# Earlier transposes for the first four head pairs, and seven filler matmuls in the start-up of a fused attention and mixer kernel

## The chip, the cores and the metric

The kernel runs on one core of one Trainium2 chip. The metric is the device time of one execution in microseconds, as the median of several runs. The span of a profile, from the first to the last instruction of the core, is some 1.7 us shorter than the time of the same run.

## The reference

Four batches of eight heads with 768 rows of 64 go through block-sparse attention (a band, the outer blocks, and sampled blocks). The result is mixed over the tokens and then over the channels.

```python
scores = scale * np.matmul(q, k.transpose(0, 1, 3, 2))      # mask: blocks of 32
scores = np.where(mask, scores, -1000000000.0)
attn = softmax(scores)                                      # cut
x = (attn @ v) laid out as [B, S, H * D]                    # cut
u = x + (np.maximum(x^T @ w_tok1, 0) @ w_tok2)^T            # token mixing
out = u + np.maximum(u @ w_ch1, 0) @ w_ch2                  # channel mixing
```

## The kernel before

The program is written by a planner. Streams of matmuls and a list of operations for ScalarE and VectorE are placed in order of time by a cost model, and what comes out is one fixed order of instructions per engine. A stream with a lower number goes first. In the early part the planner adds a margin to some streams before it takes their inputs as ready:

```python
t = self.when(deps, tags)
...                                             # cut
if self.now < self.tight:                       # the first 40 us of the plan
    t += 300.0 if 1.5 < s[0] < 2.5 else 100.0 if s[0] == 1 else 0.0
```

The start-up is written by hand. Seven long matmuls on a constant keep TensorE busy while the first inputs arrive; then come the first transposes of pair 0, the mask rows (two matmuls of 24 x 24 x 384) and eight short fillers ahead of the first scores:

```python
for i in range(7):
    idle_mm()                                   # 512 columns each
...                                             # cut: masks, loads
first_lay(acopy, "q", 0)
qt0 = first_turn("q", 0)                        # three transposes
first_lay(acopy, "k", 0)
e2a, e2b = e2_mm(0, psM, "pm"), e2_mm(0, psO, "po")     # mask rows
kt0 = first_turn("k", 0)
for i in range(8):
    idle_mm(128)
```

Every later pair is loaded, laid out anew by VectorE (relayout), transposed by TensorE and copied out of PSUM. For pairs 1 to 3:

```python
lays = relayout(p)                              # klay, qlay, vaug: copies of priority 2 and 3
...                                             # cut: twelve transposes into PSUM
ev = P.op(("dve", "act"), {"dve": 550.0, "act": 740.0}, [last], evac, prio=2)
...
P.stream(0, qk_stream())                        # scores, then exp on ScalarE
P.stream(1, pv_stream())                        # PV: probabilities times values
P.stream(2, tr_stream())                        # transposes of all pairs
P.stream(1.7, first_tok_stream((0, 1, 2)))      # token mixing of batch 0
```

The softmax here doesn't subtract the row's maximum and nothing guards it: scores larger than these inputs give would overflow.

Of the kernel before, what the change touches and what calls it, by code (L numbers as in the profile page):

```python
# [25 lines left out]
def free(base_ap: bass.AP, extra_offset: int, dims) -> bass.AP:  # L26

    return bass.AP(
        tensor=base_ap.tensor,
        offset=base_ap.offset + extra_offset,  # L30
        ap=[list(base_ap.ap[0])] + [list(d) for d in dims],
    )
# [142 lines left out]
def kernel(  # L175
# [18 lines left out]
    NP = B * H // 2  # L194
# [6 lines left out]
    NT0 = 4  # L201
# [16 lines left out]
    P = Planner({"ps": 2, "po": 1, "pm": 3, "et": NET, "a_t": 2, "o": 3, "rc": 2,  # L218
                 "uT": 3})
# [3 lines left out]
    raws, arrive = {}, {}  # L223
# [92 lines left out]
    def idle_mm(n=512):  # L316
        nc.tensor.matmul(
            out=idle_ps[:, 0, 0:n], lhsT=free(one[:, 0:1], 0, [[0, 128]]),
            rhs=free(one[:, 0:1], 0, [[0, n]]), start=True, stop=True,
        )  # L320
# [68 lines left out]
    def first_lay(copy, nm, hf):  # L389
        copy(  # L390
            out=lay0[nm][:, 3 * hf : 3 * hf + 3, :, :],
            in_=f32[nm][:, :, 3 * hf : 3 * hf + 3, :].rearrange("p h c d -> p c h d"),
        )

    def first_turn(nm, hf):
        t = psM.tile([128, 3, 128], BF16, tag="pm", name=f"t{nm}first{hf}")
        for c in range(3):
            nc.tensor.matmul(
                out=t[:, c, :], lhsT=lay0[nm][:, 3 * hf + c, :, :].rearrange("p h d -> p (h d)"),
                rhs=ident[:, :], start=(c == 0), stop=(c == 2), is_transpose=True,  # L400
            )
        return t
# [8 lines left out]
    def e2_mm(hf, pool, tag):  # L411
        t = pool.tile([128, 512], FP32, tag=tag, name=f"pm_e2_{hf}")
        nc.tensor.matmul(  # L413
            out=t[R, 0:384], lhsT=t2add[R, :], rhs=indf[:, 384 * hf : 384 * hf + 384],
            start=True, stop=True,
        )
        return t
# [4 lines left out]
    vcopy, acopy = nc.vector.tensor_copy, nc.scalar.copy  # L422
    first_lay(acopy, "q", 0)
    qt0 = first_turn("q", 0)
    first_lay(acopy, "k", 0)
    e2a, e2b = e2_mm(0, psM, "pm"), e2_mm(0, psO, "po")
    kt0 = first_turn("k", 0)
    for i in range(8):
        idle_mm(128)
    first_evac(acopy, "q", 0, 0, qt0)  # L430
    first_evac(acopy, "q", 0, 1, qt0)
# [120 lines left out]
    kT_there, qT_there, va_there, qk_done, pv_done = {}, {}, {}, {}, {}  # L552
# [5 lines left out]
    def relayout(p):  # L558
        lays = {}
        for nm in ("k", "q", "v") if p else ("v",):  # L560
            raw = raws.pop((nm, p))
            arr = arrive.pop((nm, p))

            def emit(eng, nm=nm, raw=raw):
                if nm == "v":
                    nc.vector.tensor_copy(out=vaug[p % NV][:, :, :, 0:64], in_=raw)  # L566
                else:
                    lay = sbw.tile([128, NC, 2, D], BF16, tag=f"{nm}lay", bufs=2, name=f"{nm}lay{p}")
                    nc.vector.tensor_copy(
                        out=lay[:, :, :, :], in_=raw.rearrange("p h c d -> p c h d")  # L570
                    )
                    lays[nm] = lay

            deps = [arr]
            if nm == "v" and p >= NV:
                deps.append(pv_done[p - NV])
            if nm != "v" and p >= 3:
                deps.append(qT_there[p - 2, 1])
            if nm != "v" and p >= NPE:
                deps.append(quiet[sum(p > g for g in GATES)])  # L580
            if nm != "v" and p > NV + 4:
                deps.append(qk_done[p - NV + 1])
            lays[nm + "ev"] = P.op(("dve",), {"dve": 320.0}, deps, emit, prio=2 if nm != "v" else 3)
            copied[nm, p] = lays[nm + "ev"]
        va_there[p] = lays["vev"]
        return lays

    def crossbar(p):

        lays = relayout(p)  # L590
        for nm, bufs, there in (("k", ktb, kT_there), ("q", qtb, qT_there)):
            def emit(eng, nm=nm, bufs=bufs):
                nc.sync.dma_start_transpose(
                    out=bufs[p % NV][:, 0, :].rearrange("e (c s) -> e c s", c=NC),
                    in_=lays[nm][:, :, :, :].rearrange("p c h d -> p (c h d)"),
                )
            deps = [lays[nm + "ev"], mask_there, qk_done[p - NV]]
            ev = P.op(("sp",), {"sp": 1300.0}, deps, emit, prio=1, lat=4600.0)
            there[p, 0], there[p, 1] = ev, ev

    def transposes(p):
        yield lambda: ("v", p) in raws
        if p >= NPE:
            crossbar(p)
            return
        if p == 0:
            relayout(p)
            for nm in ("k", "q"):
                copied[nm, p] = Ev(START)
            for hd in range(2):  # L610
                kT_there[p, hd], qT_there[p, hd] = f_there["k", 1], f_there["q", 1]
            yield from first_rest()
            return
        for hd in range(2):
            kT_there[p, hd], qT_there[p, hd] = Ev(), Ev()
        lays = relayout(p)
        for nm, bufs, there in (("k", ktb, kT_there), ("q", qtb, qT_there)):
            box, last, rel = {}, Ev(), Ev()
            for c in range(NC):
                def emit(nm=nm, c=c, box=box, rel=rel):  # L620
                    if c == 0:
                        P.take("pm", rel)
                        box["t"] = psM.tile([128, NC, 128], BF16, tag="pm", name=f"t{nm}{p}")
                    nc.tensor.matmul(  # L624
                        out=box["t"][:, c, :],
                        lhsT=lays[nm][:, c, :, :].rearrange("p h d -> p (h d)"),
                        rhs=ident[:, :], start=(c == 0), stop=(c == NC - 1), is_transpose=True,
                    )
                deps = [lays[nm + "ev"]]
                if p >= NV:  # L630
                    deps.append(qk_done[p - NV])
                if p >= NT0:
                    deps.append(mask_there)
                yield 56.0, deps, [("pm", 1)] if c == 0 else [], emit, last if c == NC - 1 else None
            if p >= NT0:
                def evac(eng, buf=bufs[p % NV], box=box):
                    copy = nc.scalar.copy if eng == "act" else nc.vector.tensor_copy
                    copy(out=buf[:, 0, :], in_=box["t"][:, :, :].rearrange("p c s -> p (c s)"))

                ev = P.op(  # L640
                    ("dve", "act"), {"dve": 555.0, "act": 740.0}, [last, mask_there], evac, prio=2
                )
                for hd in range(2):
                    alias(there[p, hd], ev)
                alias(rel, ev)
                continue
            for hd in range(2):
                def evac(eng, hd=hd, buf=bufs[p % NV], box=box):
                    i = box["t"][64 * hd : 64 * hd + 64, :, :].rearrange("p c s -> p (c s)")
                    if eng == "act":  # L650
                        nc.scalar.copy(out=buf[0:64, hd, :], in_=i)
                    else:
                        nc.vector.tensor_copy(out=buf[0:64, hd, :], in_=i)

                ev = P.op(("dve", "act"), {"dve": 550.0, "act": 740.0}, [last], evac, prio=2)
                alias(there[p, hd], ev)
                if hd == 1:
                    alias(rel, ev)

    def alias(a, b):  # L660
        a.same_as = b
# [420 lines left out]
        for t in range(3):  # L1082
            x_there[p, t] = Ev()

    def tr_stream():
        for p in range(NP):
            yield from transposes(p)

    def tok_stream():
# [4 lines left out]
    def first_tok_stream(pairs):  # L1094
        for p in pairs:
            yield from tok_pair(p)
# [4 lines left out]

    P.stream(0, qk_stream())
    P.stream(1, pv_stream())
    P.stream(2, tr_stream())
    P.stream(1.7, first_tok_stream((0, 1, 2)))
    P.stream(0.5, first_tok_stream((3,)))
    P.stream(3, tok_stream())
# [100 lines left out]
```

## Time and profile before

| what | before |
|---|---|
| median of the first three runs | 258.02 us |
| the profiled run, its span | 255.23 us, 253.5 us |
| TensorE busy | 97% of the span |
| ScalarE, VectorE busy | 68%, 71% |

The views that carry the reading of the steady part are in the prediction. One more is needed here, TensorE's timeline of the start-up in the kernel before (start, length, engine, line, operation, operands, count, and the idle time before it with what ended it; PE is TensorE, ACT ScalarE, DVE VectorE):

```profile
3.96 0.53 PE L398 MATMUL tqfirst<-ident,qlay_first 128*128 128x128 bf16 x3
4.58 0.74 PE L413 MATMUL pm_e<-ktb,t2add 24*24 24x384 bf16 x2
5.25 0.34 PE L398 MATMUL tkfirst<-ident,klay_first 128*128 128x128 bf16 x3
5.43 0.63 PE L317 MATMUL ps_idle<-one 128*128 128x128 bf16 x8
6.35 0.89 PE L682 MATMUL ps<-qtb,ktb 88*128 88x256 bf16 x4 [0.29 <-DVE ktb L406]
```

The length of a group contains the latency of its last matmul (here a warm transpose alone takes 0.22 us, three take 0.34), so the pitch is read from lengths of like groups: three transposes take 0.53 us at 3.96 and 0.34 at 5.25. By the trace's single records their starts stand 0.107 us apart at 3.96 and 0.056 to 0.067 at 5.25; those of the 512-column fillers before them stand 0.427 apart from the second on. The clock of the array doubled between the two groups; the trace records the switch from half to full at 5.11. Between the first transposes and the mask rows at 4.58 there is a small hole: 0.09 us between the records, and some 0.3 us by the prediction's estimate that three transposes from 3.96 are through at 4.28.

### The profile page before, as it was taken

To read this page: it belongs to the slowest core of one execution; us is meant where nothing else is said; L and a number is where in the kernel's file an instruction comes from. 1 tells how busy PE (TensorE), PEld (TensorE's weight loads), DVE (VectorE), ACT (ScalarE), POOL (GpSimd) and SP (SyncE) were. 2 spreads that over 40 slices of the span, in tenths; PEclk is the share of its full clock that TensorE was granted. 3 is DMA by queue.
4 is the path that set the end of the run, shared out by engine and by line. 5 is a ranking of instruction groups with operands and counts; after the bars stand their busy time and mean duration, and the time that the engine had idled before them with its cause. 6 is when DMAs were issued, how large, how long until landed. Compare 5 with 4: busy or idle time off the path is not lost.

```text
span 253.5 us, 6661 instructions
## 1 busy us (share of the span) xinstructions
PE 244.9 (97%) x2777; PEld 159.2 (63%) x2796; DVE 179.8 (71%) x399; ACT 173.2 (68%) x214; POOL 51.4 (20%) x88
## 2 busy tenths in 40 slices
PE   7889999999999999999999999999999999999995
PEld 3579998566666556755676565557666744566444
DVE  6987666999898898998988989898998412200222
ACT  6799999968888577777896776676976310277100
POOL 8835985006740000082000000000000000000000
PEclk9999999999999999999999999999999999999999
DMA  6999999765995971279483313710400042300122
GB/s 153 183 215 202 212 203 206 129 79 86 161 201 90 172 161 67 52 120 187 72 127 65 63 45 79 131 73 12 100 9 1 3 103 83 124 3 0 41 111 99
DMA packets 44959, 26.77 MB, mean 106 GB/s; under 512 B 25408, under 2 KB 42064, under 8 KB 44928
## 3 DMA queue, kind: packets, MB, share of 16 engines
q0 software_dynamic: 15104, 12.98, 33.3%
q1 hardware_dynamic: 29552, 13.15, 23.0%
q8 instruction: 22, 0.36, 0.6%
q10 hardware_dynamic: 272, 0.20, 0.3%
q14 instruction: 9, 0.07, 0.1%
HBM read 26.74 MB, written 6.29 MB: 130 GB/s over the span
## 4 chain that ended last, share of the span: by engine, by line
PE 90%; DVE 3%; ACT 3%; issue 2%; ACTq 0%
PE pm_ch L1020 25%; PE pm_ch L1047 24%; PE ps L682 17%; PE po L776 14%; PE pm_tok L878 3%; ACT et L692 3%; PE pm_tok L853 3%; PE pm_tok_p L963 1%; PE pm_tok_p L940 1%; DVE qtb L420 1%; PE pm_e L413 0%; DVE vaug L566 0%; DVE dkf L357 0%; PE tk L624 0%; PE pm_ut L906 0%
## 5 line engine op out<-in xcount | busy, mean ns | idle before, releaser
L692 ACT ACTIVATE et<-ps 128x1024 bf16<-128x1024 f32 x144 | 138.9, 1023 | 32.4 <-PE ps L682 30.3
L1020 PE MATMUL pm_ch<-uT,w_ch 128*128 128x384 bf16 x384 | 74.1, 326 | 0.0
L700 DVE TENSOR_TENSOR et<-et,mask 128x1024 bf16<-128x1024 bf16 x108 | 70.2, 683 | 0.7 <-ACT et L692 0.6
L1047 PE MATMUL pm_ch<-w_ch,rc 128*128 128x512 bf16 (+2 forms) x293 | 66.1, 362 | 1.0 <-issue 0.5
L776 PEld LDWEIGHTS <-et 128*128 128x128 bf16 x1152 | 50.6, 97 | 17.3 <-issue 3.0
L776 PE MATMUL po<-vaug,et 128*128 128x65 bf16 x1152 | 57.0, 193 | 1.1 <-ACT et L692 0.4
L682 PE MATMUL ps<-qtb,ktb 64*128 64x256 bf16 (+1 forms) x576 | 55.5, 272 | 2.0 <-ACT et L692 1.1
L817 ACT ACTIVATE rc<-pm_ch 128x384 bf16<-128x384 f32 x58 | 28.5, 492 | 26.3 <-PE pm_ch L1020 26.0
L1020 PEld LDWEIGHTS <-w_ch 128*128 128x128 bf16 x384 | 33.7, 97 | 20.0 <-issue 3.4
L1047 PEld LDWEIGHTS <-rc 128*128 128x128 bf16 x312 | 27.4, 98 | 25.1 <-issue 1.7
L1059 DVE TENSOR_TENSOR o<-pm_ch,x 128x512 f32<-128x512 f32 x23 | 15.9, 690 | 38.5 <-PE pm_ch L1047 38.2
L682 PEld LDWEIGHTS <-ktb 64*128 64x128 bf16 (+1 forms) x576 | 28.8, 95 | 19.0 <-issue 13.3
L819 DVE TENSOR_SCALAR rc<-pm_ch 128x384 bf16<-128x384 f32 x38 | 21.1, 554 | 6.0 <-PE pm_ch L1020 5.5
L791 DVE TENSOR_TENSOR x<-po,recip 128x256 bf16<-128x256 f32 x48 | 20.4, 424 | 1.7
L790 DVE RECIPROCAL recip<-po 128x4 f32<-128x4 f32 x48 | 8.7, 180 | 13.8 <-PE po L776 13.5
L886 DVE TENSOR_TENSOR x<-pm_tok,x 128x512 bf16<-128x512 f32 x18 | 11.9, 683 | 1.2 <-PE pm_tok L878 1.1
L878 PE MATMUL pm_tok<-a_t,w_tok 128*128 128x256 bf16 x72 | 11.1, 277 | 0.2 <-DVE x L886 0.2
L1131 POOL COPY seen<-ktb 1x1 bf16<-1x1 bf16 x2 | 0.4, 180 | 50.7 <-DMA ktb<-klay 34.5
L853 PE MATMUL pm_tok<-x,w_tok 128*128 128x256 bf16 x72 | 9.8, 273 | 0.0
L878 PEld LDWEIGHTS <-w_tok 128*128 128x128 bf16 x72 | 7.5, 128 | 2.0 <-issue 1.4
L255 POOL DMA_DIRECT2D vraw<-in_v_dram x10 | 7.4, 742 | 3.2 <-DMA qraw<-in_q_dram 1.3
L535 POOL COPY mask<-maskb 128x240 bf16<-128x240 bf16 (+1 forms) x18 | 7.6, 495 | 0.0
(104 smaller groups left out, 138.6 us busy)
## 6 DMA issues: line engine op xcount, KB each, us to landing
out_dram<-o SPq DMA_DIRECT2D x17, 256.0 KB, 2.0
w_ch<-in_moe_w_ch_dram POOLq DMA_DIRECT2D x8, 384.0 KB, 9.8
vraw<-in_v_dram POOLq DMA_DIRECT2D x10, 192.0 KB, 6.9
kraw<-in_k_dram POOLq DMA_DIRECT2D x9, 192.0 KB, 6.9
qraw<-in_q_dram POOLq DMA_DIRECT2D x9, 192.0 KB, 6.8
out_dram<-o SPq DMA_DIRECT2D x13, 128.0 KB, 1.8
w_tok<-in_moe_w_tok_dram POOLq DMA_DIRECT2D x2, 384.0 KB, 10.6
ktb<-in_v_dram POOLq DMA_DIRECT2D x3, 192.0 KB, 8.5
```

Of the source, the lines that this page charges most:

```text
L682: nc.tensor.matmul(out=ps[:, hd, 256 * i : 256 * i + 256], lhsT=ktb[n][rows, h, 256 * jj + 128 * i : 256 * jj + 128 * i + 128], rhs=qtb[n] ...
L692: nc.scalar.activation(out=et[:, :, :], in_=ps[:, :, :], func=AF.Exp, scale=0.125)
L700: nc.vector.tensor_tensor(out=ets[s][:, :, :].rearrange("k h (i q) -> k h i q", i=2), in0=ets[s][:, :, :].rearrange("k h (i q) -> k h i q" ...
L776: nc.tensor.matmul(out=po[:, hd, c, :], lhsT=et[:, hd, 256 * i + 128 * c : 256 * i + 128 * c + 128], rhs=va[:, hd, 2 * jj + i, 0:65], star ...
L791: nc.vector.tensor_tensor(out=free(xs[b][:, pb // 2, 2 * t, 128 * (pb % 2) : 128 * (pb % 2) + 128], 0, [[64, 2], [256, 2], [1, 64]],), in0 ...
L817: nc.scalar.activation(out=o(), in_=i, func=AF.Relu)
L819: nc.vector.tensor_scalar(out=o(), in0=i, scalar1=0.0, scalar2=None, op0=ALU.max)
L853: nc.tensor.matmul(out=box["pm"][:, t, :], lhsT=w_tok1[:, sc, 128 * t : 128 * t + 128], rhs=xs[b][:, g, sc, :], start=(t == 0 and sc == 0) ...
L878: nc.tensor.matmul(out=ubox["pm"][:, i, :], lhsT=w_tok2[:, t, :, 2 * s2 + i], rhs=a_t[:, t, :], start=(i == 0 and t == 0), stop=(i == 1 an ...
L1020: nc.tensor.matmul(out=pbox["pm"][:, 0:384], lhsT=w_ch1[:, dmc, 128 * cc : 128 * cc + 128], rhs=st[b]["uT"][:, dmc // 2, 3 * sh : 3 * sh + ...
L1047: nc.tensor.matmul(out=pbox["pm"][:, 0:n], lhsT=box["rc"][:, cc, 128 * sc : 128 * sc + 128], rhs=w_ch2[:, cc, lo : lo + n], start=(cc == 0 ...
L1059: nc.vector.tensor_tensor(out=o[:, :].rearrange("p (g e) -> p g e", g=2), in0=pbox["pm"][:, :].rearrange("p (g e) -> p g e", g=2), in1=st[ ...
```

## The change

The intent is to have the transposed pairs ready earlier, by moving transposes ahead of PV and their copies ahead of relayouts, and to close two small holes of the start-up with fillers. The condition on pair p-2 only keeps the two transpose streams in order.

```diff
     qt0 = first_turn("q", 0)
+    for i in range(3):
+        idle_mm(128)
     first_lay(acopy, "k", 0)
 ...
-    for i in range(8):
+    for i in range(12):
         idle_mm(128)
 ...
-        yield lambda: ("v", p) in raws
+        yield lambda: ("v", p) in raws and (p < 2 or (p - 2, 1) in qT_there)
 ...
-                ev = P.op(("dve", "act"), {"dve": 550.0, "act": 740.0}, [last], evac, prio=2)
+                ev = P.op(("dve", "act"), {"dve": 550.0, "act": 740.0}, [last], evac, prio=1.5)
 ...
-    P.stream(2, tr_stream())
+    P.stream(0.7, tr_stream(range(NT0)))
+    P.stream(2, tr_stream(range(NT0, NP)))
```

(NT0 is 4. The stream function takes the pairs as its argument; that hunk is cut.)

More of the change, by code (lines that the diff above doesn't have):

```diff
@@ L653, in evac @@
                         nc.vector.tensor_copy(out=buf[0:64, hd, :], in_=i)
-                ev = P.op(("dve", "act"), {"dve": 550.0, "act": 740.0}, [last], evac, prio=2)
+                ev = P.op(
+                    ("dve", "act"), {"dve": 550.0, "act": 740.0}, [last], evac, prio=1.5
+                )
                 alias(there[p, hd], ev)
@@ L1083, with tr_stream @@
             x_there[p, t] = Ev()
-    def tr_stream():
-        for p in range(NP):
+    def tr_stream(pairs):
+        for p in pairs:
             yield from transposes(p)
```

## The prediction

> **What bounds the kernel now.** I read three views in this order: the chain of work that ended last (which engine sets the end), the busy time by stretch (where that engine is not full), and the timelines of ScalarE, TensorE and VectorE around the emptiest stretch (what it waits for there).
>
> The chain, by engine, and then the stretches; the columns are the stretch in us, its length, and the busy us of each engine with its number of instructions:
>
> ```profile
> PE 90%; DVE 3%; ACT 3%; issue 2%; ACTq 0%
> ```
>
> ```profile
> 7.28:12.00 4.72, 3.75 (x47) 2.46 (x44) 4.42 (x10) 4.07 (x5) 4.00 (x6) 1.00 1.20 179
> 12.00:18.00 6.00, 5.58 (x100) 5.09 (x97) 5.21 (x14) 5.62 (x7) 2.89 (x4) 1.00 1.17 214
> 18.00:24.00 6.00, 5.57 (x92) 4.99 (x91) 4.52 (x13) 5.91 (x7) 3.08 (x5) 1.00 1.30 200
> 24.00:30.00 6.00, 6.00 (x106) 5.68 (x104) 3.20 (x10) 6.00 (x7) 5.14 (x12) 1.00 1.21 209
> ...
> 48.00:54.00 6.00, 5.66 (x67) 3.38 (x66) 5.72 (x16) 5.19 (x7) 0.00 (x0) 1.00 0.27 49
> 54.00:100.00 46.00, 45.59 (x567) 28.82 (x570) 41.01 (x88) 35.83 (x44) 11.63 (x17) 1.00 0.85 133
> 100.00:200.00 100.00, 99.01 (x1205) 63.68 (x1213) 86.38 (x179) 75.11 (x90) 7.29 (x11) 1.00 0.39 73
> ```
>
> TensorE is the bound: 90% of the chain is its matmuls, and from 54 to 200 us it is busy 99%. Its work is a fixed sum, so a change of order can only win what TensorE idles. Between 7.28 and 54 us that is 2.2 us (46.72 us less the 44.51 us busy in the stretches between these marks), nearly all of it before 24 us and in 48 to 54 us. The whole prize of reordering the first four pairs is therefore about 2 us, 0.8% of 258.
>
> The first four pairs run one exponential (exp) after another on ScalarE, with the matmuls fitted between. ScalarE's timeline (start, length, engine, line, operation) shows one hole:
>
> ```profile
> 11.91 4.94 ACT L692 ACTIVATE et<-ps 128x1024 bf16<-128x1024 f32 x5 [0.18 <-PE ps L682]
> 16.74 0.79 ACT L651 COPY ktb<-tk 64x768 bf16<-64x768 bf16 x1
> 17.86 4.71 ACT L692 ACTIVATE et<-ps 128x1024 bf16<-128x1024 f32 x5 [0.34 <-PE ps L682]
> ```
>
> The ninth exp, the last of pair 0, ends at 16.85; the tenth, the first of pair 1, starts at 17.86. That is 1.01 us without an exp. A transpose copy (0.79 us) lies in it, but does not make it: ScalarE then still waits 0.34 us for scores. TensorE and VectorE say why the scores are late:
>
> ```profile
> 15.85 0.65 PE L776 MATMUL po<-vaug,et 128*128 128x65 bf16 x16
> 16.91 0.42 PE L776 MATMUL po<-vaug,et 128*128 128x65 bf16 x8 [0.41 <-ACT et L692]
> 17.16 1.04 PE L682 MATMUL ps<-qtb,ktb 88*128 88x256 bf16 x8
> ```
>
> ```profile
> 10.16 0.58 DVE L566 COPY vaug<-vraw 128x768 bf16<-128x768 bf16 x1
> 10.78 0.55 DVE L488 COPY qtb<-qtb 24x1536 bf16<-24x1536 bf16 x1
> 11.36 0.59 DVE L569 COPY klay<-kraw 128x768 bf16<-128x768 bf16 x1
> ...
> 12.71 0.43 DVE L569 COPY qlay<-qraw 128x768 bf16<-128x768 bf16 x1
> 13.07 0.29 DVE L521 TENSOR_SCALAR maskb<-pm_mask 128x144 bf16<-128x144 f32 x1
> 13.32 1.12 DVE L653 COPY ktb<-tk 64x768 bf16<-64x768 bf16 x2
> ...
> 15.67 1.13 DVE L653 COPY qtb<-tq 64x768 bf16<-64x768 bf16 x2
> ```
>
> Pair 1's last transposed q is in place only at 16.80. Expecting that, the planner put the last eight PV matmuls of pair 0 ahead of pair 1's first scores; those eight wait for the ninth exp, so nothing of pair 1 can be scored before 17.16.
>
> [...]the scores at 17.16 stand behind a PV group that began to wait 0.41 us earlier. [...]the seven 512-column fillers from 1.00 take 3.17 us (about 0.43 each with the last one's tail), and later transposes stand 0.056 us apart. The new fillers are to be judged by that. [...]
>
> **The change, part by part**, with the order of instructions of both programs laid side by side.
>
> 1. Fillers: three more 128-column matmuls after the first q transposes, four more before the first scores. Before, TensorE is idle 0.1 us before the first mask-row matmul (4.58) and 0.29 us before the first scores (6.35). Three cold fillers are 3 x 0.107 = 0.32 us from about 4.29 (three transposes from 3.96 at 0.107), so until 4.61: the mask rows may go 0.03 us later. Four warm ones, 4 x 0.056 = 0.22, fit the 0.29. Cost 0 to 0.05 us. If they brought the warm clock forward, the two mask-row matmuls would gain at most 0.3 us (384 columns, 3 x 0.107 = 0.32 each, halved); I give that little weight, since TensorE was all but full there already.
>
> 2. Pair 1 earlier. VectorE's new order is row copy, vaug, maskb, klay, qlay, two ktb copies, reciprocal and normalisation, two qtb copies. With the start-to-start times of before: the row copy at 10.16 (+0.58), vaug 10.74 (+0.62), maskb 11.36 (+0.25), klay 11.61 (+0.59), qlay 12.20 (to 12.63). The k transposes are split around a score group on TensorE and end near 13.2; ktb copies 13.3 (+1.04), reciprocal and product (+0.56) to 14.9, qtb copies (1.13) to 16.0. So pair 1 stands at about **16.0 instead of 16.8**, and its first scores now follow a PV group whose exp is long done. They issue at about 16.1, and the tenth exp starts as the ninth ends, at about 16.85: **1.0 us earlier**. The hole of 0.18 at 11.9 may close too, since the fifth score group of pair 0 now goes ahead of sixteen PV matmuls that it stood behind; but one k transpose waits for klay (12.2) ahead of the next score group, which may open 0.15 again. I count these as nil.
>
> 3. Copies ahead of relayouts: ScalarE no longer does the 0.79 us copy; VectorE does it (0.55). That is no further gain, the copy lay in the hole already counted. In exchange four eviction ReLUs go from ScalarE to VectorE (58 and 38 become 54 and 42).
>
> 4. What reaches the end. The channel mixing can start once pair 3 is token-mixed, in the trace at 50.23; from there TensorE is full. In the new order it starts after the 45th score group, not the 44th. One group more costs about 0.96 us of exp rhythm (17 in 16.30 us), so the start is near 50.23 - 1.0 + 0.9 = about 50.1. But the extra score group (0.33 us of TensorE by start-to-start) and eight to sixteen more PV matmuls (0.25 to 0.5) are then done. Sum: 0.1 + 0.33 + 0.4 = 0.8, to which the 0.26 us wait at 49.3, perhaps filled by the extra work, could add. I take **0.9 us**: 258.02 - 0.9 = 257.1.
>
> **Rivals.** *The hole moves instead of closing*: transposes now stand in TensorE's queue ahead of PV and without the planner's margin of 0.3 us, so a late relayout blocks scores as well. For it: klay and qlay stand behind vaug and maskb, and VectorE is 5.21 of 6 us busy there. Against: half a microsecond of slack by step 2. It would leave 257.5 to 258.2. *Transfers set the pace*: the input queues move some 200 GB/s until 48 us, and VectorE waited 1.3 us for pair 3's k at 21.39. Against: pair 3 is scored only at 34, so the exps have slack; 0.2 us lost at most. *VectorE becomes the bound later*: it is 86% busy from 100 to 200 us and gets some 2.8 us more (four ReLUs at 0.55 and a copy). Against: TensorE idles only 1 us in those 100 us. *The plan shifts everywhere*: every later step is placed anew, with other transfers in between; TensorE idles some 1.4 us in 54 to 200 now, and a redraw can add or save as much. This is the largest term of the range, and the likeliest way to see no gain. *Everything idle goes*: 2.2 us, 255.8, is the floor.
>
> **Range and chances.** Centre 257.1; downward to the floor, 255.8; upward, the gain lost and 0.5 us of new stalls on top, 258.5. Faster by 2% would need 5.2 us, over twice the idle time there is; slower by 2% needs as much in new stalls, which only a badly wrong plan gives. Hence 0.02, 0.96, 0.02.
>
> **What would show it.** Right: in ScalarE's timeline the tenth exp starts at 16.7 to 17.1 with no copy in the exp phase; pair 1's qtb copies end near 16.0; TensorE's idle time from 12 to 24 us falls from 0.85 to under 0.4; 54 to 200 us stays as full as before. Wrong: a wait of a score group for a relayout or a transposed copy near 12 to 16 us, an exp hole elsewhere before 50 us, a start of channel mixing after 50.3, or more than 2 us of TensorE idle in 54 to 200. A gain over 2 us would mean that busy TensorE time hid more slack than its records show.

## The result, and the profile after

The changed kernel took 254.41 us (median of four runs, 254.26 to 255.08); before, beside it, took 258.03 (257.66 to 259.83). The ratio is 0.9851 with a 95% interval of 0.9802 to 0.9900. A ratio is always the mean time of one kernel's fast runs over that of the other's in the same rounds, so it is not quite the ratio of the medians. That is 3.6 us, four times the predicted 0.9 and below the predicted range. Chance made it larger: none of these four runs of before was a quick one, where 16 of all 46 are (table below). The mean of all 46 is 257.44, against 254.94 for all ten runs of the changed kernel, 2.5 us apart.

The two profiles tell another tale: the spans are 253.5 and 252.6 us, 0.9 apart. First the busy time by stretch of the changed kernel, in the columns of the prediction's table:

```profile
12.00:18.00 6.00, 5.68 (x103) 5.21 (x100) 5.03 (x14) 5.92 (x8) 2.86 (x4) 1.00 1.18 215
18.00:24.00 6.00, 6.00 (x106) 5.52 (x103) 5.04 (x14) 6.00 (x7) 3.24 (x5) 1.00 1.30 201
...
48.00:54.00 6.00, 6.00 (x58) 3.43 (x57) 5.71 (x15) 5.42 (x9) 0.00 (x0) 1.00 0.40 44
54.00:100.00 46.00, 45.73 (x559) 27.84 (x562) 41.27 (x88) 32.99 (x39) 11.13 (x17) 1.00 0.80 136
100.00:200.00 100.00, 99.52 (x1212) 63.25 (x1217) 87.19 (x182) 75.45 (x90) 6.81 (x11) 1.00 0.38 72
```

TensorE idles 0.32 us from 12 to 24 us, where it idled 0.85, and 0.75 us from 54 to 200, where it idled 1.40. ScalarE's timeline of the changed kernel has no hole and no copy from the second exp on:

```profile
7.51 1.02 ACT L696 ACTIVATE et<-ps 128x1024 bf16<-128x1024 f32 x1 [0.99 <-PE ps L686]
9.11 41.87 ACT L696 ACTIVATE et<-ps 128x1024 bf16<-128x1024 f32 x44 [0.57 <-PE ps L686]
```

VectorE's last copies for pair 1, in the changed kernel, end at 16.09 instead of 16.80:

```profile
14.96 1.13 DVE L655 COPY qtb<-tq 64x768 bf16<-64x768 bf16 x2
```

And TensorE's start-up in the changed kernel, with the new fillers:

```profile
4.29 0.53 PE L317 MATMUL ps_idle<-one 128*128 128x128 bf16 x3
4.74 0.81 PE L413 MATMUL pm_e<-ktb,t2add 24*24 24x384 bf16 x2
5.49 0.50 PE L398 MATMUL tkfirst<-ident,klay_first 128*128 128x128 bf16 x3
5.78 0.95 PE L317 MATMUL ps_idle<-one 128*128 128x128 bf16 x12
6.59 0.89 PE L686 MATMUL ps<-qtb,ktb 88*128 88x256 bf16 x4
```

Here the array is still at half clock at 5.49 (three transposes in 0.50 us; the trace records the switch at 5.94), so in this run the first scores are even 0.24 us later than in the profiled run of before. So the profiles show the reordering at work, and a gain of 0.9. The other 2.7 us lie between the profiled run of before (255.23) and its usual runs (258). Something differs from run to run of one and the same program.

### The profile page after: what moved, and what is told of

Its sections match the earlier page's. It is cut to its first block, busy times and chain, and to the rows that moved or that the text cites.

```text
span 252.6 us, 6684 instructions
## 1 busy us (share of the span) xinstructions
PE 246.2 (97%) x2786; PEld 158.6 (63%) x2803; DVE 182.5 (72%) x404; ACT 169.8 (67%) x209; POOL 50.1 (20%) x88
## 4 chain that ended last, share of the span: by engine, by line
PE 95%; DVE 2%; ACT 2%; issue 1%
PE pm_ch L1024 25%; PE pm_ch L1051 24%; PE ps L686 17%; PE po L780 15%; PE pm_tok L882 4%; PE pm_tok L857 3%; ACT et L696 2%; PE ps_idle L317 1%; PE pm_tok_p L967 1%; PE pm_tok_p L944 1%; PE pm_ut_p L990 1%; DVE qtb L420 1%; PE tq L626 1%; DVE ktb L406 1%; PE tk L626 1%
## 5 line engine op out<-in xcount | busy, mean ns | idle before, releaser
L1024 PE MATMUL pm_ch<-uT,w_ch 128*128 128x384 bf16 x384 | 73.0, 326 | 0.1
L780 PEld LDWEIGHTS <-et 128*128 128x128 bf16 x1152 | 48.1, 97 | 14.3 <-issue 3.8
L780 PE MATMUL po<-vaug,et 128*128 128x65 bf16 x1152 | 55.2, 193 | 0.2
L821 ACT ACTIVATE rc<-pm_ch 128x384 bf16<-128x384 f32 x54 | 26.6, 492 | 25.7 <-PE pm_ch L1024 25.6
L1051 PEld LDWEIGHTS <-rc 128*128 128x128 bf16 x312 | 28.0, 98 | 24.6 <-issue 0.2
L823 DVE TENSOR_SCALAR rc<-pm_ch 128x384 bf16<-128x384 f32 x42 | 23.3, 554 | 5.9 <-PE pm_ch L1024 5.2
```

Of the source, the lines that this page charges most:

```text
L780: nc.tensor.matmul(out=po[:, hd, c, :], lhsT=et[:, hd, 256 * i + 128 * c : 256 * i + 128 * c + 128], rhs=va[:, hd, 2 * jj + i, 0:65], star ...
L821: nc.scalar.activation(out=o(), in_=i, func=AF.Relu)
L823: nc.vector.tensor_scalar(out=o(), in0=i, scalar1=0.0, scalar2=None, op0=ALU.max)
L1024: nc.tensor.matmul(out=pbox["pm"][:, 0:384], lhsT=w_ch1[:, dmc, 128 * cc : 128 * cc + 128], rhs=st[b]["uT"][:, dmc // 2, 3 * sh : 3 * sh + ...
L1051: nc.tensor.matmul(out=pbox["pm"][:, 0:n], lhsT=box["rc"][:, cc, 128 * sc : 128 * sc + 128], rhs=w_ch2[:, cc, lo : lo + n], start=(cc == 0 ...
```

## The experiments

All kernels below gave correct results. Each list of runs is in the order of time. All are labelled fast but for some at 259.2 us or more, which are called slow only because they lie over 1.5% above the fastest run of the same kernel; on one core there is no second die to compare with. A call that held quick runs of before thus loses its slowest from the ratio, so I compare levels of single runs and not the ratios.

The theories: **A**, the reordering saves, and the fillers only pad; **B**, the fillers decide when TensorE gets its full clock, which usual runs of before get late. The later texts call B the clock theory.

### Fillers alone, and the reordering alone (first call)

Before plus both groups of fillers:

```diff
+    for i in range(3):
+        idle_mm(128)
-    for i in range(8):
+    for i in range(12):
```

> The kernel before with both groups of fillers (3 and 4 more) and nothing else. Theory A, the reordering is what saves: no change, 257.5 to 258.5 us. Theory B, the fillers bring TensorE to its full clock reliably, and a usual run of before (258.0, against 255.2 in its one profiled run) misses it: 254.8 to 255.6 us, the time of that profiled run.

Measured: 255.40, 255.31, 255.27, 256.69. Before in the same rounds: 259.66, 254.83, 259.85, 254.91, 258.24, 258.13, 255.14. Theory A's 258 is out. The fillers take away the upper levels without any reordering.

The changed kernel minus the same seven fillers (the diff above, reversed):

> The changed kernel without its seven new fillers: the reordering alone. Theory A: 254.2 to 254.8 us, as the whole change. Theory B: 256.5 to 257.5 us, 1 us under before, since the profiles differ by 0.9 us in span.

Measured: 255.17, 255.07, 257.14, 256.69; neither theory's numbers fit all four. The profiled run (255.17) shows why. Its stretches between 12 and 16 us have the granted clock in the third column from the end:

```profile
12.00:14.00 2.00, 2.00 (x21) 1.75 (x19) 0.16 (x2) 1.18 (x2) 1.42 (x3) 0.50 1.29 199
14.00:16.00 2.00, 1.68 (x23) 1.36 (x21) 1.77 (x5) 1.54 (x3) 1.05 (x2) 0.93 1.10 244
```

TensorE had its full clock from 4.06 us (the transposes there take 0.36 us instead of 0.53) and fell back to half from 10.88 to 14.30, for 3.4 us (score groups take 1.06 us at 12.24 and 0.60 at 14.97). So there are two ways to lose: a late warm-up, and a relapse. The mean clock of a run gives the relapses away: 0.993 is 0.007 x 253 us at half lost, so 1.8 us lost or 3.5 us at half clock. (A mean of 0.998 need not be a relapse: in the result's profile it is the fall at 251.70, just before the end.)

The kept traces hold the times of the clock's switches, which the views do not print. In fifteen of the 17 the first switch lies between 3.64 and 6.97 us; in the two late ones it lies at 16.56 and 20.40. It differs from run to run of one program: the two profiles of before itself have it at 5.11 (the first one) and at 3.64 (the one of the third call). What sets it was not shown.

Before plus the three fillers in the first hole only:

```diff
     qt0 = first_turn("q", 0)
+    for i in range(3):
+        idle_mm(128)
```

> The kernel before with the three fillers between the first transposes and the mask rows alone. Theory A: 257.5 to 258.5 us. Theory B with the gap of 0.1 us before the mask rows as the culprit: near 255.3 us; with the gap before the first scores as the culprit: still 258.

Measured: 254.75, 255.49, 254.77, 254.90.

Before plus the four fillers ahead of the first scores only:

```diff
-    for i in range(8):
+    for i in range(12):
```

> The kernel before with the four fillers before the first scores alone (12 in place of 8). Theory A: 257.5 to 258.5 us. Theory B: near 255.3 us if the gap before the first scores (0.29 us) is the culprit, 258 if it is the one before the mask rows.

Measured: 258.25, 255.56, 260.09, 254.98. The three fillers after the first transposes are the ones that matter; the other four leave the levels as they were. The profiled run of this kernel fell on a late one (258.25), and TensorE's timeline shows it at work:

```profile
5.61 1.49 PE L317 MATMUL ps_idle<-one 128*128 128x128 bf16 x12
...
14.49 1.03 PE L682 MATMUL ps<-qtb,ktb 88*128 88x256 bf16 x4
15.32 0.85 PE L624 MATMUL tk<-ident,klay 128*128 128x128 bf16 x6
...
17.33 0.60 PE L682 MATMUL ps<-qtb,ktb 88*128 88x256 bf16 x4
```

A score group takes 1.03 us at 14.49 and 0.60 at 17.33; between them, by the trace at 16.56, the clock came. Before it the score groups of four take 1.01 to 1.06 us and six transposes 0.85 (at 15.32; 0.50 at 18.63), and between the exps from 7.99 to 17.12 ScalarE waits 0.18 to 1.00 us for scores. The clock column says 1.00 for the stretches from 0 to 18 us all the same, so this late warm-up must be read from the lengths.

### Which part does what (second call)

The changed kernel with 8 in place of 12 fillers before the first scores:

```diff
-    for i in range(12):
+    for i in range(8):
```

> The changed kernel with the three gap fillers but 8 instead of 12 fillers before the first scores. The gap fillers alone on before measured 254.8, both groups 255.3, so if the four tail fillers cost 0.5 us by delaying the first scores: 253.8 us, all runs within 1.3 us. If the tail fillers help to keep the clock: 254.4 with some runs over 256.

Measured: 254.22, 257.01, 254.43, 255.41, with clocks of 0.999, 0.987, 1.000 and 0.993. A miss: the best run is not better than with 12, and there were two relapses, of some 6.6 us at half clock (257.01) and 3.5 (255.41) by these means. With four runs it can't be told whether the four fillers made the difference.

The changed kernel with 6 in place of 7 long warm-ups, so that the hole moves ahead of the first transposes:

```diff
-    for i in range(7):
+    for i in range(6):
         idle_mm()
```

> The changed kernel with 6 in place of 7 long warm-up fillers, which leaves TensorE idle for some 0.4 us before the first transposes. Theory clock [...]: the slow runs return, several of four at 256.5 us or more, with matmuls at the doubled pitch beyond 6 us. Rival, the fillers only pad and the spread is chance: 254.2 to 254.6 in all runs, as nothing waits for the seventh filler.

Measured: 255.25, 257.96, 257.77, 255.09. All other fillers and the reordering are in place, and nothing waits for the seventh warm-up; still half the runs are back at 258. This is what theory B said of the times. The doubled pitch beyond 6 us was not seen, as the profiled run (255.25) was a quick one: a hole of 0.16 us before the first transposes, full clock from 4.10, and a relapse from 10.93 (mean clock 0.993, so some 3.5 us at half; a score group takes 1.06 us at 12.21 and 0.60 at 14.97).

The changed kernel with only the transposes moved, copies at their old priority:

```diff
-                    ("dve", "act"), {"dve": 550.0, "act": 740.0}, [last], evac, prio=1.5
+                    ("dve", "act"), {"dve": 550.0, "act": 740.0}, [last], evac, prio=2
```

> The changed kernel with the transposes ahead of PV, but their copies at the old priority. The order up to pair 1's copies is that of the whole change, so the hole before the tenth exp closes: 254.2 to 254.6 us if this half of the reordering saves the 1.0 us; 255.3 if the copies' priority does.

Measured: 255.28, 255.99, 255.27, 255.84. The hole before the tenth exp is closed, and yet nothing is won. ScalarE's timeline of this kernel:

```profile
9.11 21.08 ACT L696 ACTIVATE et<-ps 128x1024 bf16<-128x1024 f32 x22 [0.56 <-PE ps L686]
30.50 1.94 ACT L696 ACTIVATE et<-ps 128x1024 bf16<-128x1024 f32 x2 [0.31 <-PE ps L686]
32.60 10.64 ACT L696 ACTIVATE et<-ps 128x1024 bf16<-128x1024 f32 x11 [0.16 <-PE ps L686]
43.76 8.36 ACT L696 ACTIVATE et<-ps 128x1024 bf16<-128x1024 f32 x9 [0.52 <-PE ps L686]
```

Three holes of together 0.99 us open later in the same exp phase. Channel mixing starts at 50.66, against 49.80 in the changed kernel. The gain was given back before it reached the end.

The changed kernel with only the copies moved, transposes at the old priority:

```diff
-    P.stream(0.7, tr_stream(range(NT0)))
+    P.stream(2, tr_stream(range(NT0)))
```

> The changed kernel with the copies ahead of relayouts, but the transposes at the old priority behind PV. The order up to pair 1's copies is that of before, so the hole of 1 us stays: 255.3 us, as with the fillers alone; 254.4 if the copies' priority is what saves.

Measured: 256.56, 255.96, 256.03, 255.55, all with clock 1.00. The old hole is there, and channel mixing starts only at 51.50. In the profiles of this call and of the changed kernel, only both halves together keep the exps without a hole. Why these four runs differ by 1 us at a full clock I did not find out.

### The relapses, and the levels themselves (third call)

The changed kernel with eight more fillers where TensorE waits 0.67 us for an exp, ahead of the fourth score group. To be tested is whether the relapses come from this wait. The wait in TensorE's timeline of the changed kernel:

```profile
10.19 0.90 PE L686 MATMUL ps<-qtb,ktb 88*128 88x256 bf16 x4 [0.67 <-ACT et L696]
```

The edit:

```diff
         p, t, jj = s
+        if s == (0, 1, 0):
+            hole = psO.tile([128, 512], FP32, tag="po", name="po_hole")
+            for i in range(8):
+                nc.tensor.matmul(out=hole[:, 0:128], lhsT=<ones>, rhs=<ones>, start=True, stop=True)
         P.take("ps", rel)
```

> The changed kernel with eight more fillers in the hole of 0.67 us before the fourth score group of pair 0, where TensorE waits for an exp. Theory clock: the relapses to half clock after the warm-up (runs at 255.1 us with a mean clock of 0.993, 257.0 with 0.987) [...]; with it filled all runs are at 254.2 to 254.7 with clocks of 0.998 or more. Rival, relapses have another cause: one to three of six runs at 255 to 257 us, as before.

Measured: 254.83, 254.69, 254.94, 254.60, 255.12, 255.06; all clocks 0.999 or 1.000. TensorE's timeline of this kernel, where the wait for the exp has shrunk to 0.21:

```profile
9.35 0.63 PE L682 MATMUL po_hole<-one 128*128 128x128 bf16 x8
10.19 0.90 PE L693 MATMUL ps<-qtb,ktb 88*128 88x256 bf16 x4 [0.21 <-ACT et L703]
```

The changed kernel itself in the same rounds:

> The changed kernel itself, for the share of its levels: most runs at 254.2 to 254.6 us, a few at 255 to 257 with a clock of 0.985 to 0.994 [...], none with a late warm-up.

Measured: 254.53, 255.55, 254.87, 255.42, 255.51, 255.34, with clocks of 0.999, 0.993, 1.000, 0.992, 0.992, 0.993. Four of six runs relapsed, by their clocks for some 3.5 to 4 us at half, and took 255.3 to 255.6, where the two without took 254.5 and 254.9. I had expected a few. With the hole filled none of six did. No late warm-up in either, as expected.

Before without its seven warm-ups:

```diff
-    for i in range(7):
+    for i in range(0):
         idle_mm()
```

> The kernel before without its seven long warm-up fillers, so that TensorE starts cold and with holes. Theory clock: every run has a late full clock and lands with the slow runs of before or worse, 257.5 to 261 us, with matmuls at the doubled pitch to 10 us or beyond. Rival, the two levels of before (255 and 258 to 260) have nothing to do with the warm-up: still two levels, some runs at 255.

Measured: 259.99, 259.66, 259.24, 259.72. The two levels are gone, and what is left is the upper one, with transposes still at the long pitch at 19 us (three in 0.51 us; the first switch is at 20.40). The upper level of before, 259.3 to 259.9, lies where a start without any warm-up lies.

Before itself:

> The kernel before itself, for the share of its levels: half the runs at 254.6 to 255.3 us, the others at 257.7 to 258.3 or 259.5 to 259.9. If the profiled run is one of the slow ones, its trace shows matmuls at the doubled pitch until beyond 12 us and the same order of waits after that.

Measured: 257.68, 257.96, 259.37, 258.73, 258.08, 259.25; no quick run among six, against half expected. The profiled run (257.68, clock 0.987) was not the late warm-up that I expected but one that relapsed for 6.8 us:

```profile
10.00:12.00 2.00, 2.00 (x25) 1.63 (x25) 1.40 (x3) 1.40 (x2) 1.43 (x2) 0.62 1.31 199
12.00:14.00 2.00, 2.00 (x23) 1.61 (x22) 1.09 (x4) 1.18 (x2) 1.43 (x2) 0.50 1.28 191
14.00:16.00 2.00, 2.00 (x26) 1.75 (x24) 1.50 (x4) 1.09 (x2) 0.73 (x2) 0.50 1.15 254
16.00:18.00 2.00, 2.00 (x26) 1.71 (x24) 0.44 (x3) 1.34 (x2) 0.70 (x1) 0.68 1.11 200
```

Half clock from 10.47 to 17.29, and ScalarE (fourth engine) busy 1.1 to 1.4 of every 2 us: its exps waited for scores. A busy TensorE here is a slow one, not a productive one: score groups take 1.04 us at 14.70 and 0.60 at 17.63. So no late warm-up of before itself was profiled: for its other slow runs it is read from their mean clocks, which show no relapse, and from the profile of the kernel with the late fillers.

### The reordering at a settled clock (fourth call)

What was left open is the reordering's own worth, as all comparisons so far mix clock phases. With all three holes filled in both, before and the changed kernel:

```diff
 (the kernel before)
+    for i in range(3):                     # after the first q transposes
+        idle_mm(128)
-    for i in range(8):
+    for i in range(12):                    # before the first scores
+        if s == (0, 1, 0):                 # and the eight into po_hole, as above
```

> The kernel before with all fillers of the change and the eight more in the hole before the fourth score group: the old order at a settled clock. If the reordering is worth 0.9 us on its own: 255.7 us, 0.9 above the next run. If it is worth 0.4 or less: 254.9 to 255.3. No run over 256.5 either way, as the clock theory has no late warm-up and no relapse here.

Measured: 254.66, 255.26, 255.37, 255.36, 254.76, 254.74 (mean 255.03).

The changed kernel with the same holes filled, the file of the third call again:

```diff
 (the changed kernel)
+        if s == (0, 1, 0):                 # the eight into po_hole, as above
```

> The changed kernel with the same eight fillers (e9 again, for the same rounds): 254.6 to 255.1 us in all runs.

Measured: 254.74, 255.12, 254.97, 254.52, 255.00, 254.59 (mean 254.82). No run of either relapsed or warmed up late. The reordering is worth **0.2 us** here, the difference of two means whose runs spread by 0.6 to 0.7; it is not clear of zero. In the profiled runs both spans are 253.0. The changed order (the last run named) shows a hole which its first profile did not have, in ScalarE's, TensorE's and VectorE's timelines:

```profile
31.56 19.83 ACT L703 ACTIVATE et<-ps 128x1024 bf16<-128x1024 f32 x21 [0.56 <-PE ps L693]
```

```profile
30.61 0.42 PE L787 MATMUL po<-vaug,et 128*128 128x65 bf16 x8 [0.40 <-DVE x L802]
```

```profile
26.35 0.70 DVE L571 COPY klay<-kraw 128x768 bf16<-128x768 bf16 x1
...
28.46 1.54 DVE L568 COPY vaug<-vraw 128x768 bf16<-128x768 bf16 x2
```

The relayouts, which now come after the copies, fall between 26 and 30 us. There they take twice as long as elsewhere or longer: klay 0.70 us instead of 0.35, and the two vaug copies 1.54 instead of 0.62 at 20.01. The normalisation after them comes late, PV waits 0.40 us for it, and the scores behind PV wait too. In the first profile of the changed kernel the same copies were a little shorter (0.55, and 1.44 for the two) and the hole did not open; GpSimd spreads the masks there from 25.80 to 28.48 and issues loads from 28.43 to 30.59. Whether the copies are long because of GpSimd's work was not tested.

This hole sets a limit to the 0.2. It stands near 31 us in all three profiles of the changed order with the eight fillers (0.56, 0.56 and 0.61 us; spans 253.1, 253.0 and 253.0) and in none of the three at full clock without them (spans 252.6, 252.8 and 252.5). The old order's shortest spans are 253.1 with the gap fillers and 253.0 with all. So 0.2 is the worth of the reordering beside the eight fillers; by the profiles without the hole it is some 0.2 to 0.6. Whether the eight fillers open the hole was not tested.

The last run also drops the four fillers ahead of the first scores:

```diff
-    for i in range(12):
+    for i in range(8):
```

> The same with 8 in place of 12 fillers before the first scores. If the four tail fillers delay the first scores where the full clock comes late (first scores at 7.02 instead of 6.59 us in two profiles): 0.1 to 0.4 us under the run before. If they are needed for the clock: some runs at 255.4 or more with a clock under 0.995.

Measured: 254.73, 253.65, 254.53, 255.03, 254.57, 254.26 (mean 254.46), no clock under 0.998. It is 0.36 us below the run before, as expected, though the runs of this one spread by 1.4, so this is not clear of the noise. By its mean it is quicker than before (254.46 against 256.67 for the eleven runs of before in these rounds) and than the changed kernel (254.94 over its ten runs, of two other calls): the version to keep, if one had to choose.

### All runs together

| kernels | runs | 253.6 to 257.2 us | 257.6 us and more |
|---|---|---|---|
| before | 46 | 16 | 30 |
| no warm-ups at all | 4 | 0 | 4 |
| before with the four late fillers only | 4 | 2 | 2 |
| six warm-ups | 4 | 2 | 2 |
| the reordering without fillers | 4 | 4 | 0 |
| seven warm-ups and the three gap fillers, in either order | 54 | 54 | 0 |

The four runs of the reordering without fillers leave a rival, that the reordering alone takes the upper level away. Its two runs at 256.69 and 257.14, with clocks of 0.999, may be late warm-ups that cost less in this order, and neither was profiled. That the reordering does not keep the upper level away is shown by the kernel with six warm-ups, which contains it and has two of four runs there.

## Why the prediction was right or wrong, point by point

**The starting point** was the first mistake. The text subtracted 0.9 us from 258.02, the median of the timed runs, after reading all of its idle times from a run of 255.23. The two numbers stood side by side. A profiled run that is 2.8 us quicker than the others is a run in which something that costs 2.8 us is missing; the bound on the prize ("about 2 us, 0.8% of 258") was read from a trace that did not contain the loss.

**The fillers** are the step that failed, in its own words: "If they brought the warm clock forward, the two mask-row matmuls would gain at most 0.3 us [...]; I give that little weight, since TensorE was all but full there already." The mechanism was named, and its size was taken from two matmuls. The clock is not won for two matmuls but for all that run until it comes, which in the late run with the four late fillers was at 16.56 us. Without the gap fillers, 30 of 46 runs of before lay 2.7 to 5 us above its quick level of 254.9, by a late clock or a long relapse, as far as profiles and mean clocks tell; with them 54 of 54 runs of nine kernels stayed under 257.1. Added alone to before, both groups of fillers gave 255.3 to 256.7 and the first three alone 254.8 to 255.5, in rounds in which four of seven runs of before took 258.1 to 259.9. The cost given for them was small but low as well: where the fillers ran cold, the mask rows started at 4.74 instead of 4.58 (0.16 us, not 0.03), and the four late ones cost 0.36 us by the means of the last call and 0.5 by the medians of the first (255.35 against 254.84), neither clear of the spread, and nothing that could be told in the second.

**Pair 1 earlier** held: its copies end at 16.09 (predicted 16.0), the tenth exp starts at 16.84 (predicted 16.85), and the hole before the tenth exp is gone, together with the copy on ScalarE. (One reading is loose: the PV group waited 0.41 us before its own start at 16.91, so its wait began 0.66 us before the scores at 17.16, not 0.41.) The hole of 0.18 us at 11.9 closed too, and none opened in that profile. The rival of a VectorE that becomes the bound did not come: TensorE idles less from 54 to 200 us than before.

**What reaches the end** looked right and is doubtful. Channel mixing starts at 49.80 (predicted about 50.1), and the spans of the two profiled runs differ by the predicted 0.9. But with all holes filled the same two orders differ by 0.2. So 0.9 was the worth of one pair of runs; the step that treated 1.0 us of exp rhythm as won left out that a later hole can take it back, which it does in the run with the transposes alone (0.99 us) and in all three profiles of the whole order with the eight fillers (0.56 to 0.61). The rival "the hole moves instead of closing" describes this; it was argued only for the first 16 us, though the signs of being wrong named an exp hole anywhere before 50 us, and it came at 30 to 44.

**The floor.** "Everything idle goes: 2.2 us, 255.8, is the floor" fails because a busy TensorE at half clock takes longer for the same work (a score group 1.03 us against 0.60). Idle time bounds what a reordering can win only where the clock is the same. The prediction's last line named this case, a gain over 2 us, but the range gave it no room.

**The chances** held: the change is clear of noise in its median but within 2% (ratio 0.9851).

What stays open: why the first switch differs from run to run (3.64 to 6.97 us in fifteen traces, 16.56 and 20.40 in two), and why the same hole of about 0.3 us near 4.4 us leaves 16 of 46 runs of before quick and 30 not. The wait of 0.67 us between 8.8 and 10.2 us also came before a relapse in some runs only: the three profiled relapses began 6.8 us after a first switch at 3.64 to 4.10 us, while seven profiles with the same wait unfilled and a first switch at 4.63 to 6.92 kept it, and so did one at 4.01. Of the four profiles with the wait filled only one had a first switch that early (4.17); it kept the clock.

## What to carry to other kernels

Before reading a profile, hold the profiled run against the other runs: if it is not one of them, it does not contain what is to be explained. Where the time of one program has levels several us apart, look at the lengths of equal matmuls in the first 20 us (here 1.03 us against 0.60 for a score group), not at the clock column (1.00 in both places) or the busy share. Try fillers in TensorE's first holes, before it has its full clock and after: here all 54 runs with seven warm-ups and three of them near 4.3 us stayed under 257.1 us, where 30 of 46 of before took 257.6 and more, and eight in the wait of 0.67 us took the relapses from four of six runs to none of six. A hole closed early on the side of another engine is worth something only if the same trace, and a second one, shows none opening later.
